# Spectral mixer and gated FFN on one core: remainder transform in 64 by 64 tiles, masked products on 128 partitions, a new middle order, and two weight slots loaded later

## Chip, core and metric

One core of a Trainium2 chip runs the whole program. The metric is the device time of one execution in microseconds. The kernel before ran three times: 489.95, 490.86 and 492.05 us, median 490.86. A fourth execution was profiled: 489.82 us, of which the span from its first to its last recorded instruction is 487.8 us. The granted TensorE clock was 1.000 throughout.

## What is computed

```
x = A_x                                    # 1 x 2048 x 576
X = rfft2(layernorm(x)) * (w_r + 1j*w_i)   # w: 2048 x 289
h = x + irfft2(X)
y = h + (gelu(n @ w_gate) * (n @ w_up)) @ w_down,   n = layernorm(h)
# w_gate, w_up: 576 x 4608, w_down: 4608 x 576; all bf16
```

## The kernel before

The token axis of 2048 is split as 128 by 16 in the program's Fourier transforms, the channel axis of 576 into halves, and every transform is a matmul with a constant table. The program is written by hand as one list of operations per engine; a small recorder (class Prog) keeps, for each operation, which keys it reads and writes, and from these it works out the semaphore waits. Each engine executes its list strictly in the order in which the operations were recorded. So the order of the calls in the source is the order on each engine.

The stages, with their times in the profiled execution:

1. *Start, to about 20 us.* x arrives, layernorm statistics, and a first token transform (line 552) into U.
2. *Middle, about 20 to 46 us.* The order is the string SEQF (line 28), a list of tokens with a letter and a group number 0 to 15. A capital letter is the first half of a step, the small letter its second half:
   - D/d, st_D (line 636): channel transform, U times FT into two PSUM banks (line 640), then copied to CUS.
   - B, st_B (line 655): combination matmuls (line 660), then copied to YS.
   - T, st_T (line 664): VectorE multiplies YS by the spectral weights WS: 256 columns into TP, the remaining 32 columns of each group into TR (line 673). Four groups share one TR buffer.
   - V/v, st_V (line 676): token transform of TP (line 681), then copied to V.
   - R/r, st_R (line 692): the same transform for the remainder of four groups, TR times VT (line 697). Its PSUM result is copied to RB by ScalarE, and VectorE then multiplies RB by a 0/1 mask MK into VR (line 711), so that each group's rows stand alone.
   DENG, BENG and VENG (lines 29 and 30) say for each group whether ScalarE, VectorE or both make the copy of D, B and V. Copies all stand in line 607. The 128-partition by 512-column PSUM banks are handed out in four pairs by a loop over SEQF (line 592).
3. *Inverse, about 46 to 59 us.* The order is the string SEQ (line 33). I/i (line 808) transforms V and VR over channels, E copies the result to GS, N/o (line 825) transforms over tokens, a adds the result to x in XO (line 831). Then the second layernorm of the first four token tiles: s, q, c, n (lines 834 to 858; the norms with the letter P run on GpSimd), u/U (line 877) turns the tile by a matmul with the unit matrix, e copies it to HT. G0 and G1 are the first matmuls of the FFN.
4. *FFN, from 58.61 us.* Four blocks of 512 tokens; in each, 36 columns of 128 hidden units (line 917, gate and up), Gelu on ScalarE, product on VectorE, and then the down product (line 1004). In the first block the inverse of the other eight token tiles is woven in (deferred, lines 962 and 979).

In stage 2 and 3 a matmul uses 64 contraction rows: two of them, on rows 0 to 63 and 64 to 127, write two different PSUM banks. The second half of a step swaps the rows and adds to the other bank, and so waits for the first half (halves, line 612).

The weights of gate and up lie in four slots of nine hidden columns (1152 units) each. wg_load (line 629) issues for one slot two DMAs of w_gate from GpSimd's queue and two of w_up from SyncE's queue, 1.18 MB and 0.15 MB each. Slot 0 is issued at line 750. Slots 1 and 2 use the space of WS and its copies, so they wait for the last multiplication of st_T; they are issued at line 772, in the program's order between the middle and the inverse. w_down follows on GpSimd's queue (line 946), slot 0 is loaded anew at line 1024 once its nine columns are done in the first block.

Of the kernel before, what the change touches and what calls it, by code (L numbers as in the profile page):

```python
# [7 lines left out]
ALU = mybir.AluOpType  # L8
# [18 lines left out]
ACT_TILES = tuple(int(w[1:]) for w in SEQ1 if w[0] == "Q")  # L27
SEQF = """D1 D0 d1 D2 d0 d2 B1 D4 B0 d4 D3 T1 B2 T0 d3 D5 V1 d5 T2 v1 D6 B3 d6 B4 V0 B5 T3 v0 D7 T4 D8 d7 B6 d8 V3 R0 T5 v3 T6 r0 V2 B7 v2 D9 V5 d9 D10 v5 d10 V4 B9 T7 D12 v4 d12 B8 D11 T9 B10 d11 R1 D13 T8 T10 r1 d13 D14 B11 V6 d14 V7 v6 v7 T11 B12 V8 D15 v8 B13 T12 d15 B14 T13 V9 v9 T14 R2 r2 B15 V10 V12 v10 V13 v12 R3 T15 r3 V11 v13 V14 v11 v14 V15 R4 v15 r4""".split()
VENG = [('act',), ('dve',), ('act',), ('act',), ('act', 'dve'), ('act', 'dve'), ('act', 'dve'), ('act', 'dve'), ('act',), ('act',), ('act',), ('act',), ('act',), ('act',), ('act', 'dve'), ('act', 'dve')]
DENG, BENG = ['act', 'act', 'dve', 'act', 'act', 'act', 'dve', 'act', 'dve', 'act', 'act', 'act', 'dve', 'act', 'act', 'dve'], ['act', 'act', 'act', 'act', 'act', 'act', 'act', 'act', 'act', 'act', 'act', 'act', 'act', 'act', 'act', 'act']  # L30
QR = ((0, 1), (1, 2), (2, 3), (3, 4), (4, 8), (8, 16))
# [298 lines left out]
def _build(nc, A_x, A_w_r, A_w_i, B_w_gate, B_w_up, B_w_down, out):  # L330
# [91 lines left out]
    def bank(b, p0=0, p1=128, c0=0, c1=512):  # L422
        return PS[p0:p1, b * 512 + c0:b * 512 + c1]
# [185 lines left out]

    turn_over = {}  # L610

# [80 lines left out]
    def st_R(q, second):  # L692
        js = [i for i in range(4 * q, 4 * q + 4) if i < LAST] if q < 4 else [LAST]
        g0, n, b0 = GORD[js[0]], len(js), FB["R", q]

        def mm(h, o, t_, first, last, after):
            return P.op(PE, lambda t: t.matmul(bank(b0 + o, 0, 128, 0, 128), TR[64 * h:64 * h + 64, q % 2, o, t_, :], VT[64 * h:64 * h + 64, 1 + o if q == 4 else 0, t_, :], start=first, stop=last),
                        r=[("TR", q % 2, j) for j in range(4)] + ["VT"], w=[("PS", b0 + o)], after=after)

        halves(("R", q), second, [[0, 1]] * 2, mm)  # L700
        if not second:
            return
        ev(ACT, RB[:, q % 2, :, :, :, :].rearrange("p t n o e -> p o (t n) e"), banks(b0, 2, 128).rearrange("p o (a e) -> p o a e", e=4),
           [("PS", b0), ("PS", b0 + 1)], [("RB", q % 2)])
        for u in range((n + 1) // 2):
            m = min(2, n - 2 * u)
            for t_ in range(2):
                dst = VR[64 * t_:64 * t_ + 64, :, g0 + 2 * u:g0 + 2 * u + m, :, :].rearrange("p n g o e -> p n g (o e)")
                src = RB[64 * u:64 * u + 64, q % 2, t_, :, :, :].rearrange("p n o e -> p n (o e)").unsqueeze(2).to_broadcast([64, NT, m, 8])
                msk = MK[64 * u:64 * u + 64, 0:m, :].unsqueeze(1).to_broadcast([64, NT, m, 8])  # L710
                P.op(DVE, lambda v, dst=dst, src=src, msk=msk: v.tensor_tensor(dst, src, msk, op=ALU.mult),  # L711
                     r=[("RB", q % 2), "MK"], w=[("V", GORD[i], 2 + t_) for i in js[2 * u:2 * u + m]])

# [57 lines left out]
    P.alias(sum(wkeys, []) + sum(dup, []), [("WG", j, k) for j in (1, 2) for k in range(4)])  # L771
    for j in range(1, 3):
        wg_load(j, j)
    P.alias(["FT", "BT", "VT"], [("HT", 0, i, k) for i in range(4) for k in range(5)])

    vmain = [("V", g, c) for g in range(NG) for c in range(2)]
    vtail = [("V", g, c) for g in range(NG) for c in range(2, 4)]
    vk = [vmain, vmain, vtail]
# [4 lines left out]
    for t, w in enumerate(SEQ):  # L783
# [12 lines left out]
        elif k == "G":  # L796
            ing = True
            assert not held & {0, 1}

    ends = {}  # L800

# [60 lines left out]
    def turn_dma(c):  # L862
# [3 lines left out]
        for k in range(5):  # L866
            P.dma(SP, HT[:, k, 128 * (c % 4):128 * (c % 4) + 128], HN[:, hs, 128 * k:128 * k + 128], f"tr{c}",
                  r=[("HN", hs, 0), ("HN", hs, 1)], w=[("HT", q % 2, c % 4, k)], transpose=True)

    def turn_mm(c, second):  # L870
        hs, b0, e = c % 4, SLOT["u", c], ends.setdefault(("u", c), [None, None])
        plan = ((3, 0), (4, 1)) if second else ((0, 2), (1, 3), (2, 4))
        for j, ks in enumerate(plan):
            for r, k in enumerate(ks):
                r0, a = 64 * r, b0 * 512 + 192 + 128 * k + 64 * r
                o = a // 512 - b0
                e[o] = P.op(PE, lambda t, r0=r0, k=k, a=a: t.matmul(PS[:, a:a + 64], HN[r0:r0 + 64, hs, 128 * k:128 * k + 128], IDT[r0:r0 + 64, r0:r0 + 64], start=True, stop=True),
                            r=[("HN", hs, 0), ("HN", hs, 1), "IDT"], w=[("PS", b0 + o)], after=[e[o]] if second and j == 0 else [])
# [50 lines left out]
    def gu_first(i):  # L929
        for a in range(4):  # L930
# [5 lines left out]
           "e": turn_ev, "G": gu_first}  # L936
    for w in SEQ:
        a = w[1:]
        RUN[w[0]](*((int(a[:-1]), a[-1]) if a[-1] in "ADSP" else (int(a),)))

    P.alias(ukeys + [("CU", a) for a in range(3)], [("WD", j) for j in range(8)])

# [136 lines left out]
```

## Time and profile before

| | us or share |
|---|---|
| median of three runs | 490.86 |
| profiled execution, its span | 489.82, 487.8 |
| TensorE busy | 479.1 (98%) |
| VectorE, ScalarE, GpSimd busy | 188.6, 147.2, 43.2 |
| first matmul of the inverse (line 808) | 46.24 |
| first residual add (line 831) | 49.74 |
| first FFN matmuls on the chain of waits (line 917) | 58.61 |
| last w_up part of slot 1: issue, landing | 44.81, 59.34 |
| last w_up part of slot 2: issue, landing | 46.23, 70.83 |
| first matmul that reads slot 1, slot 2 | 76.33, 95.30 |

Times are counted from the first recorded instruction. A matmul's busy time includes its way through the array, so that neighbours overlap: start to start says what the array is occupied for. A weight load (PEld) belongs to every matmul and runs beside the one ahead of it. "issue" as the cause of a wait is time in which the engine waited for nothing that the profile shows. In the profile's DMA part, queue q1 is the one that SyncE's issues go through, q0 that of GpSimd's, and the packets of kind "instruction" are the engines' own programs being fetched.

### The profile page before, as it was taken

How to read it: one execution, taken by the hardware profiler on the slowest of the kernel's cores; microseconds unless marked ns; L12 is line 12 of the kernel's file. 1: busy time of each engine (PE TensorE's matmuls, PEld its weight loads, DVE VectorE, ACT ScalarE, POOL GpSimd, SP SyncE). 2: the span in 40 equal slices, each digit the busy share in tenths (PEclk: the TensorE clock that was granted, in tenths of full speed). 3: DMA queues.
4: the chain of work that ended last, by engine and by line, in shares of the span. 5: the costliest groups of instructions: out<-in, count | busy, mean ns of one | idle time of the engine just before them, and what ended most of it. 6: DMA issues, size and time to landing. Idle time of an engine off the chain costs nothing.

```text
span 487.8 us, 10721 instructions
## 1 busy us (share of the span) xinstructions
PE 479.1 (98%) x4791; PEld 286.9 (59%) x4792; DVE 188.6 (39%) x389; ACT 147.2 (30%) x294; POOL 43.2 (9%) x77
## 2 busy tenths in 40 slices
PE   7998999999999999999999999999999999999998
PEld 3876675555577744444577644444677444444775
DVE  7898746666511134333311144333211233333011
ACT  6997754343400022233200022332100123323000
POOL 5852631000300000000000000000000000000000
PEclk9999999999999999999999999999999999999999
DMA  8969998211350000100000001000000000000000
GB/s 283 231 160 321 353 329 270 74 26 26 110 170 20 16 18 19 23 1 1 1 19 19 13 20 23 15 1 2 6 19 19 7 1 1 1 0 1 13 19 18
DMA packets 25533, 32.65 MB, mean 67 GB/s; under 512 B 11664, under 2 KB 18096, under 8 KB 25488
## 3 DMA queue, kind: packets, MB, share of 16 engines
q1 hardware_dynamic: 22048, 18.27, 13.0%
q0 software_dynamic: 3440, 13.70, 8.8%
q8 instruction: 37, 0.61, 0.5%
q14 instruction: 8, 0.07, 0.1%
HBM read 26.01 MB, written 2.36 MB: 58 GB/s over the span
## 4 chain that ended last, share of the span: by engine, by line
PE 91%; DVE 3%; DMA 2%; POOL 2%; ACT 1%; issue 1%; DVEq 0%; POOLq 0%
PE PS L917 57%; PE PS L1004 29%; PE PS L537 1%; DMA WS<-WS 1%; DVE TP L673 1%; DVE XO L831 1%; DMA WS<-in_A_w_r_dram 1%; ACT U L563 1%; PE PS L962 1%; POOL WS L725 1%; POOL WS L240 1%; PE PS L808 0%; DVE VR L711 0%; PE PS L979 0%; PE PS L825 0%
## 5 line engine op out<-in xcount | busy, mean ns | idle before, releaser
L917 PE MATMUL PS<-HT,WG 64*128 64x512 bf16 (+1 forms) x2142 | 233.5, 372 | 0.0
L917 PEld LDWEIGHTS PS<-HT,WG 64*128 64x128 bf16 x2142 | 109.8, 94 | 111.0 <-issue 0.9
L925 ACT ACTIVATE GL<-PS 128x512 bf16<-128x512 f32 x144 | 85.7, 596 | 282.4 <-PE PS L917 274.4
L926 DVE TENSOR_TENSOR AT<-GL,PS 128x512 bf16<-128x512 bf16 x144 | 98.8, 687 | 165.1 <-ACT GL L925 165.1
L1004 PE MATMUL PS<-WD,AT 128*128 128x288 bf16 (+2 forms) x1152 | 141.8, 286 | 0.0
L1004 PEld LDWEIGHTS PS<-WD,AT 128*128 128x128 bf16 x1152 | 111.0, 98 | 31.5 <-ACT GL L925 1.3
L1007 DVE TENSOR_TENSOR OS<-PS,XO 128x288 bf16<-128x288 f32 (+2 forms) x32 | 14.6, 458 | 123.3 <-PE PS L1004 123.3
L917 PE MATMUL PS<-HT,WGX 64*128 64x512 bf16 x486 | 53.4, 376 | 0.0
L917 PEld LDWEIGHTS PS<-HT,WGX 64*128 64x128 bf16 x486 | 23.7, 94 | 28.8
L640 PE MATMUL PS<-FT,U 64*128 64x288 bf16 x160 | 14.1, 284 | 0.3 <-DVE V L607 0.2
L834 ACT ACTIVATE OS<-XO,NM 128x576 bf16<-128x576 bf16 x14 | 10.8, 774 | 11.4 <-DVE XO L983 11.4
L681 PE MATMUL PS<-VT,TP 64*128 64x128 bf16 x256 | 11.2, 217 | 0.1
L673 DVE TENSOR_TENSOR TP<-YS,WS 128x1024 bf16<-128x1024 bf16 x16 | 11.0, 689 | 0.4 <-ACT YS L607 0.2
L240 POOL DMA_DIRECT2D WD<-in_B_w_down_dram x9 | 6.8, 759 | 49.1 <-PE PS L979 49.1
L563 ACT ACTIVATE U<-PS 128x384 bf16<-128x384 f32 (+2 forms) x31 | 10.5, 427 | 1.4 <-PE PS L552 1.3
L495 DVE BATCH_NORM_STATS2 ST<-XO 128x6 f32<-128x288 bf16 x26 | 10.0, 441 | 1.9 <-DMA XO<-in_A_x_dram 1.7
L607 ACT ACTIVATE YS<-PS 128x576 bf16<-128x576 f32 x16 | 10.1, 661 | 0.3 <-PE PS L660 0.2
L552 PE MATMUL PS<-ATS,XO 128*128 128x128 bf16 x96 | 8.1, 219 | 1.9 <-POOL ATS L521 1.7
L681 PEld LDWEIGHTS PS<-VT,TP 64*128 64x128 bf16 x256 | 8.4, 94 | 2.1 <-PE PS L681 0.2
L537 PE MATMUL PS<-ZD 128*128 128x512 bf16 x19 | 7.5, 560 | 1.5 <-POOL ZD L430 1.5
L552 PEld LDWEIGHTS PS<-ATS,XO 128*128 128x128 bf16 x96 | 6.9, 98 | 3.1 <-POOL ATS L521 2.5
L640 PEld LDWEIGHTS PS<-FT,U 64*128 64x128 bf16 x160 | 7.0, 94 | 2.7 <-DVE V L607 0.7
(83 smaller groups left out, 213.5 us busy)
## 6 DMA issues: line engine op xcount, KB each, us to landing
WD<-in_B_w_down_dram POOLq DMA_DIRECT2D x9, 576.0 KB, 13.1
WG<-in_B_w_gate_dram POOLq DMA_DIRECT2D x4, 1152.0 KB, 9.8
WG<-in_B_w_up_dram SPq DMA_DIRECT2D x4, 1152.0 KB, 9.4
out_dram<-OS SPq DMA_DIRECT2D x30, 72.0 KB, 1.6
XO<-in_A_x_dram SPq DMA_DIRECT2D x3, 576.0 KB, 7.2
WGX<-in_B_w_up_dram SPq DMA_DIRECT2D x1, 1152.0 KB, 5.6
WGX<-in_B_w_gate_dram POOLq DMA_DIRECT2D x1, 1152.0 KB, 9.9
HT<-HN SPq DMA_TRANSPOSE x60, 2.4
```

The source lines that it names most:

```text
L240: fn = lambda e: e.dma_start(out_ap, in_ap)
L537: P.op(PE, lambda t: t.matmul(bank(b), ZD[:, 0:128], ZD[:, :], start=True, stop=True), r=["ZD"], w=[("PS", b)])
L552: P.op(PE, lambda t, b=b, lhs=lhs, p0=p0, p1=p1, s=s, e=e, o=o, c=c: t.matmul(bank(b, p0, p1, o, o + 128), lhs, ATS[:, c, :], start=s, sto ...
L563: fn = (lambda v: v.tensor_copy(dst, src)) if eng == DVE else (lambda a: a.activation(dst, src, ACTF.Copy))
L640: return P.op(PE, lambda t: t.matmul(bank(b0 + o, 0, 128, 0, 2 * HK), U[64 * h:64 * h + 64, us, 2 * i:2 * i + 2, :, :], FT[64 * h:64 * h + ...
L673: P.op(DVE, lambda v, dst=dst, y4=y4, w4=w4: v.tensor_tensor(dst, y4, w4, op=ALU.mult), r=[("Y", sl), *dup[(i >= 5) + (i >= 8) + (i >= 12) ...
L681: return P.op(PE, lambda t: t.matmul(bank(b0 + o, 0, 128, 128 * c, 128 * c + 128), TP[64 * h:64 * h + 64, z, o, t_, c:256:2], VT[64 * h:64 ...
L917: op = P.op(PE, lambda t, h0=h0, kt=kt, wt=wt, b=b, s=(not second and j == 0), e=(second and j == n - 1): t.matmul(bank(b, 0, 128, c0, c1) ...
L925: P.op(ACT, lambda a: a.activation(GL[:, s2, :], bank(b0), ACTF.Gelu_apprx_tanh), r=[("PS", b0)], w=[("GL", s2)])
L926: P.op(DVE, lambda v: v.tensor_tensor(AT[:, f, :], GL[:, s2, :], bank(b0 + 1), op=ALU.mult), r=[("GL", s2), ("PS", b0 + 1)], w=[("AT", f)])
L1004: P.op(PE, lambda t, b=b, d0=d0, d1=d1, f=f, p=p: t.matmul(bank(b, 0, 128, 0, d1 - d0), AT[:, f, 128 * p:128 * p + 128], WD[:, f, d0:d1], ...
L1007: P.op(DVE, lambda v, b=b, d0=d0, d1=d1, p=p, c=c: v.tensor_tensor(OS[:, p % 2, d0:d1], bank(b, 0, 128, 0, d1 - d0), XO[:, c, d0:d1], op=A ...
```

## The change

- *Remainder transform.* st_R no longer multiplies 64 rows by 128 columns of TR: each of its matmuls becomes four, with 64 columns of TR (u) by 64 of VT (z), each writing 64 partitions and 64 columns of its bank: the block of u and z goes to partition half z and column half u, where it went to partition half u and column half z before. 8 matmuls per step become 32. So the two token halves z of a pair of groups stand on the two partition halves, as in VR.
- *Masked products.* Therefore line 711, which made one product per pair of groups and token half on 64 partitions, makes one per pair on 128 partitions. Two keys per group of VR become one.
- *Order.* SEQF, VENG, DENG and BENG are new. SEQ is the same.
- *Loads.* Slots 1 and 2 are issued behind the whole list SEQ, and SyncE and GpSimd first wait for the last TensorE operation recorded ahead of G0. On GpSimd the three norms of SEQ then stand ahead of these loads, on SyncE the order is the same.

```diff
--- before.py
+++ after.py
@@ -25,9 +25,9 @@
 LORD = "x0-2 x2-4 a0-4 x4-8 a4-8 x8-12 x12-16 a8-16".split()
 SPLIT = tuple(int(w[1:-1]) for w in SEQ1 if w[0] == "F")
 ACT_TILES = tuple(int(w[1:]) for w in SEQ1 if w[0] == "Q")
-SEQF = """D1 D0 d1 D2 d0 d2 B1 D4 B0 d4 D3 T1 B2 T0 d3 D5 V1 d5 T2 v1 D6 B3 d6 B4 V0 B5 T3 v0 D7 T4 D8 d7 B6 d8 V3 R0 T5 v3 T6 r0 V2 B7 v2 D9 V5 d9 D10 v5 d10 V4 B9 T7 D12 v4 d12 B8 D11 T9 B10 d11 R1 D13 T8 T10 r1 d13 D14 B11 V6 d14 V7 v6 v7 T11 B12 V8 D15 v8 B13 T12 d15 B14 T13 V9 v9 T14 R2 r2 B15 V10 V12 v10 V13 v12 R3 T15 r3 V11 v13 V14 v11 v14 V15 R4 v15 r4""".split()
-VENG = [('act',), ('dve',), ('act',), ('act',), ('act', 'dve'), ('act', 'dve'), ('act', 'dve'), ('act', 'dve'), ('act',), ('act',), ('act',), ('act',), ('act',), ('act',), ('act', 'dve'), ('act', 'dve')]
-DENG, BENG = ['act', 'act', 'dve', 'act', 'act', 'act', 'dve', 'act', 'dve', 'act', 'act', 'act', 'dve', 'act', 'act', 'dve'], ['act', 'act', 'act', 'act', 'act', 'act', 'act', 'act', 'act', 'act', 'act', 'act', 'act', 'act', 'act', 'act']
+SEQF = """D0 D2 d0 D1 d2 d1 B0 T0 D5 B2 d5 D3 B1 d3 D4 V0 T2 T1 d4 v0 D6 B3 d6 B4 D7 B5 T3 d7 V1 T4 D8 v1 d8 V3 T5 V2 v3 v2 B7 D10 B6 d10 R0 T7 T6 V5 r0 v5 D9 B10 d9 D11 B8 d11 D13 B9 d13 V4 D12 v4 T8 B11 T10 d12 D14 B13 T9 d14 V6 R1 v6 T11 r1 B12 V8 D15 v8 d15 T13 V7 V9 v7 T12 R2 v9 r2 V13 B14 v13 T14 V10 B15 V12 v10 T15 v12 V11 V14 v11 v14 V15 R3 v15 R4 r3 r4""".split()
+VENG = [('dve',), ('act',), ('act',), ('act', 'dve'), ('act',), ('act',), ('act', 'dve'), ('act',), ('act',), ('act', 'dve'), ('act',), ('act', 'dve'), ('act',), ('act', 'dve'), ('act', 'dve'), ('act', 'dve')]
+DENG, BENG = ['act', 'dve', 'act', 'act', 'act', 'act', 'dve', 'act', 'act', 'dve', 'act', 'dve', 'dve', 'act', 'act', 'act'], ['act', 'act', 'act', 'act', 'act', 'act', 'act', 'dve', 'act', 'act', 'act', 'act', 'act', 'act', 'act', 'act']
 QR = ((0, 1), (1, 2), (2, 3), (3, 4), (4, 8), (8, 16))
 DEF0, DSTEP = 3, 4
 SEQ = """I3 I1 i3 I2 E3S i1 i2 E1S N3 I0 o3 i0 a3 N1 E2A N2 E0S o1 I7 a1 s3A o2 N0 i7 o0 q3 s1A a2 c3 I5 a0 E7A s2D I6 q1 i5 E5A c1 s0D i6 E6A N7 I4 o7 n3P i4 q2 a7 n1P u3 q0 N5 U3 E4A c0 o5 e3A c2 u1 n2P U1 e1A N6 n0D u0 o6 U0 N4 a5 u2 e0A a6 U2 o4 G0 e2D a4 G1""".split()
@@ -607,7 +607,7 @@
         fn = (lambda v: v.tensor_copy(dst, src)) if eng == DVE else (lambda a: a.activation(dst, src, ACTF.Copy))
         P.op(eng, fn, r=r, w=w)
 
-    turn_over = {}
+    turn_over, ends = {}, {}
 
     def halves(key, second, plans, mm):
 
@@ -693,23 +693,26 @@
         js = [i for i in range(4 * q, 4 * q + 4) if i < LAST] if q < 4 else [LAST]
         g0, n, b0 = GORD[js[0]], len(js), FB["R", q]
 
-        def mm(h, o, t_, first, last, after):
-            return P.op(PE, lambda t: t.matmul(bank(b0 + o, 0, 128, 0, 128), TR[64 * h:64 * h + 64, q % 2, o, t_, :], VT[64 * h:64 * h + 64, 1 + o if q == 4 else 0, t_, :], start=first, stop=last),
-                        r=[("TR", q % 2, j) for j in range(4)] + ["VT"], w=[("PS", b0 + o)], after=after)
-
-        halves(("R", q), second, [[0, 1]] * 2, mm)
+        e = ends.setdefault(("R", q), [[None, None], [None, None]])
+        for t_ in range(2):
+            for u in range(2):
+                for z in range(2):
+                    for h in range(2):
+                        o, r0, z0 = h ^ second, 64 * h, 64 * z
+                        e[o][z] = P.op(PE, lambda t, o=o, r0=r0, z0=z0, t_=t_, u=u: t.matmul(bank(b0 + o, z0, z0 + 64, 64 * u, 64 * u + 64), TR[r0:r0 + 64, q % 2, o, t_, 64 * u:64 * u + 64],
+                                                                                             VT[r0:r0 + 64, 1 + o if q == 4 else 0, t_, z0:z0 + 64], start=(not second and t_ == u == 0), stop=(second and t_ == u == 1)),
+                                       r=[("TR", q % 2, j) for j in range(4)] + ["VT"], w=[("PS", b0 + o)], after=e[o] if second and t_ == u == z == 0 else [])
         if not second:
             return
-        ev(ACT, RB[:, q % 2, :, :, :, :].rearrange("p t n o e -> p o (t n) e"), banks(b0, 2, 128).rearrange("p o (a e) -> p o a e", e=4),
+        ev(ACT, RB[:, q % 2, :, :, :, :].rearrange("p u n o e -> p o (u n) e"), banks(b0, 2, 128).rearrange("p o (a e) -> p o a e", e=4),
            [("PS", b0), ("PS", b0 + 1)], [("RB", q % 2)])
         for u in range((n + 1) // 2):
             m = min(2, n - 2 * u)
-            for t_ in range(2):
-                dst = VR[64 * t_:64 * t_ + 64, :, g0 + 2 * u:g0 + 2 * u + m, :, :].rearrange("p n g o e -> p n g (o e)")
-                src = RB[64 * u:64 * u + 64, q % 2, t_, :, :, :].rearrange("p n o e -> p n (o e)").unsqueeze(2).to_broadcast([64, NT, m, 8])
-                msk = MK[64 * u:64 * u + 64, 0:m, :].unsqueeze(1).to_broadcast([64, NT, m, 8])
-                P.op(DVE, lambda v, dst=dst, src=src, msk=msk: v.tensor_tensor(dst, src, msk, op=ALU.mult),
-                     r=[("RB", q % 2), "MK"], w=[("V", GORD[i], 2 + t_) for i in js[2 * u:2 * u + m]])
+            dst = VR[:, :, g0 + 2 * u:g0 + 2 * u + m, :, :].rearrange("p n g o e -> p n g (o e)")
+            src = RB[:, q % 2, u, :, :, :].rearrange("p n o e -> p n (o e)").unsqueeze(2).to_broadcast([128, NT, m, 8])
+            msk = MK[:, 0:m, :].unsqueeze(1).to_broadcast([128, NT, m, 8])
+            P.op(DVE, lambda v, dst=dst, src=src, msk=msk: v.tensor_tensor(dst, src, msk, op=ALU.mult),
+                 r=[("RB", q % 2), "MK"], w=[("V", GORD[i], 2) for i in js[2 * u:2 * u + m]])
 
     def dup_w(k, jp, pl=slice(0, 2), eng=None):
         a, b = 64 * jp, 64 - 64 * jp
@@ -769,12 +772,10 @@
 
 
     P.alias(sum(wkeys, []) + sum(dup, []), [("WG", j, k) for j in (1, 2) for k in range(4)])
-    for j in range(1, 3):
-        wg_load(j, j)
     P.alias(["FT", "BT", "VT"], [("HT", 0, i, k) for i in range(4) for k in range(5)])
 
     vmain = [("V", g, c) for g in range(NG) for c in range(2)]
-    vtail = [("V", g, c) for g in range(NG) for c in range(2, 4)]
+    vtail = [("V", g, 2) for g in range(NG)]
     vk = [vmain, vmain, vtail]
     vkeys = vmain + vtail
 
@@ -797,8 +798,6 @@
             ing = True
             assert not held & {0, 1}
 
-    ends = {}
-
     def i_mm(c, second):
         b, e = SLOT["I", c], ends.setdefault(("I", c), [None, None])
         for j in range(2 + second):
@@ -866,6 +865,8 @@
         for k in range(5):
             P.dma(SP, HT[:, k, 128 * (c % 4):128 * (c % 4) + 128], HN[:, hs, 128 * k:128 * k + 128], f"tr{c}",
                   r=[("HN", hs, 0), ("HN", hs, 1)], w=[("HT", q % 2, c % 4, k)], transpose=True)
+
+    gate_op = []
 
     def turn_mm(c, second):
         hs, b0, e = c % 4, SLOT["u", c], ends.setdefault(("u", c), [None, None])
@@ -935,9 +936,15 @@
            "s": lambda c, e: sq(c, ENG[e]), "q": ln2_q, "c": ln2_c, "n": lambda c, e: norm(c, ENG[e]), "u": lambda c: turn_mm(c, False), "U": lambda c: turn_mm(c, True),
            "e": turn_ev, "G": gu_first}
     for w in SEQ:
+        if w == "G0":
+            gate_op.append(P.ops[PE][-1])
         a = w[1:]
         RUN[w[0]](*((int(a[:-1]), a[-1]) if a[-1] in "ADSP" else (int(a),)))
 
+    for eng in (SP, POOL):
+        P.op(eng, None, after=[gate_op[0]])
+    for j in range(1, 3):
+        wg_load(j, j)
     P.alias(ukeys + [("CU", a) for a in range(3)], [("WD", j) for j in range(8)])
 
     def wd_load(j):
```

## Prediction

> **What bounds the kernel now.** I read the page first, then the chain of waits, then two windows of it instruction by instruction.
>
> The page: TensorE carries the run, and most of it lies in two lines that never wait.
>
> ```profile
> q8 instruction: 37, 0.61, 0.5%
> ...
> L917 PE MATMUL PS<-HT,WG 64*128 64x512 bf16 (+1 forms) x2142 | 233.5, 372 | 0.0
> ...
> L1004 PE MATMUL PS<-WD,AT 128*128 128x288 bf16 (+2 forms) x1152 | 141.8, 286 | 0.0
> ```
>
> The last number is idle time before the group: 0.0. From 58.61 us on the chain of waits is these two lines and the deferred columns, back to back, until 485.55. So the change can move only the start of that stretch, unless a weight comes late in it. Everything is decided before 58.61.
>
> The chain between 43 and 59 us (start, length, what):
>
> ```profile
> 43.52 0.70 DVE TP L673
> ...
> 45.36 0.75 DVE V L607 x2
> 46.10 0.14 issue
> 46.24 1.89 PE PS L808 x28
> 48.13 0.54 issue
> 48.67 0.30 PE PS L808 x2
> ...
> 49.74 0.76 DVE XO L831
> ...
> 55.55 0.62 DVE HN L858 x2
> ...
> 58.61 1.41 PE PS L917 x23
> ```
>
> VectorE ends the middle (46.10), TensorE begins the inverse (46.24), and from 49.74 to 56.17 VectorE works without a hole. What moves the first residual add (49.74) moves 58.61, and the end, by as much. The edits have to be priced at that add. "issue" at 48.13 is a stall with no semaphore behind it.
>
> The window 20.09 to 46.24 (sum, then busy time of PE, PEld, DVE, ACT, POOL, clock, DMA share, GB/s):
>
> ```profile
> 20.09:46.24 26.15, 24.76 (x522) 18.58 (x521) 25.03 (x66) 24.41 (x52) 11.97 (x22) 1.00 0.82 233
> ```
>
> Three engines are full at once. VectorE has 1.1 us of holes.
>
> **VectorE and ScalarE in the middle.** Line 711 ran 18 times on 64 partitions, 14 of 256 elements (0.284 us) and 4 of 128 (0.22): 4.86 us. On 128 partitions there are 7 and 2, 2.43 us, if the time goes by elements in a partition: TR on 128 partitions (128x128) takes 0.220, VR on 64 (64x128) 0.221. So -2.43. The new engine lists put one YS copy on VectorE (+0.76, as its 128x576 CUS copies) and split seven V copies, not six (+0.42). Net -1.25 us. ScalarE: one YS (0.66) and one whole V (0.60) less, one half V (0.42) more: -0.84.
>
> **TensorE in the middle.** 40 matmuls of line 697 become 160 of 64x64. A call of four took 0.112 us (34.527 to 34.639). The nearest row is line 877, whose moving side also has 64 columns: a pair each 0.0285, so 16 in 0.23. Bounds: four tiles at once, 0.11; one after the other as in line 552 (0.056 each), 0.90. I take 0.23: +0.12 on each of 10 calls, 1.2. A change of array shape shows three times: 19.943 to 20.095 where the spacing was 0.055, 133.411 to 133.720 for 0.216, 168.888 to 169.106 for 0.122, each about 0.10 more. The new order has eight stretches of these calls, 16 changes: 1.5. So +2.7 us of TensorE; ends 0 and 9.4.
>
> [...]
>
> So work that VectorE loses (1.25) comes back on TensorE, whose starts alone (160 and 64 matmuls at 0.061, 296 at 0.028) already take 22.0 us of 26.15.
>
> **The instruction blocks.** Each added matmul also brings a weight load: 240 more TensorE instructions ahead of the inverse. The 37 packets of q8 hold 16,384 bytes each. Laid beside the trace, one belongs to every 256 TensorE instructions; block limits fall at 192 + 256 n in the count of executed instructions. The stall at 48.13 ends exactly on such a limit (number 1472), and that instruction has no wait in the program. Packet times against the instant when TensorE passes a limit: 29.11, packet 31.08; 35.37, 38.85; 41.68, 46.05; 48.66, 52.55; in the quiet dense part the packet comes 1.9 us before. So with full DMA queues (1.00 from 40 to 44 us) a packet is 3.5 to 4.4 us late; it takes 1.2 and TensorE resumed 1.43 after it: 6.2 to 7.0 us from one limit until the next block can run. Before, a block lasted 6.3 us (22.68, 29.11, 35.37, 41.68): just enough, and once not.
>
> [...]
>
> After, limits fall by the built order as follows. T8 still waits for its copied weights (landed 34.40), so the ninth T starts at 34.45 as before. Limit 960 lies ahead of it, in V4 and D12, about 33.9. Limit 1216 lies in v7, which T12 needs. VectorE from 34.45: five T (0.75 each), one CUS copy (0.76), half a V (0.42), two VR (0.57): T12 at 39.95. The block behind 1216 is asked for at 33.9 and there at 40.1, so v7 runs then and T12 slips to about 40.4. Limit 1472 lies in v11, three calls behind v10, which T15 needs. From T12 to T15 VectorE has T12 and T14 (1.5), two half V (0.84), two VR (0.57): T15 at 43.3, v11 due about 44. But the block asked for at 40.1 is there at 46.3 to 47.1: a stall of 2.3 to 3.1 us where nothing is buffered any more. The weights moved away don't help: their issue was at 44.39. From v11 to the first inverse matmul are 184 instructions with V15, v15 and four R calls: 1.9 us by the same end of before (44.37 to 46.24), plus 0.3 for two shape changes. Inverse at 48.5 to 49.3. The next limit, 1728, falls about 2 us into the inverse; its packet is asked for at about 46.7 with the queue nearly empty (what is left of slot 0's weights and two tables landed by 49.35 even with the later weights in between), so I take no stall, where before had 0.54. Add at 46.24-to-49.74 without the stall, 2.96 later: 51.5 to 52.3 against 49.74, +1.8 to +2.5. I take the low end, **+1.8**, since the packet is late by 3.5 more often than by 4.4.
>
> **Weights of slots 1 and 2 behind the inverse.** Eight issues (SP 3.3 us, POOL 2.7) go from 44.39 to the last matmul ahead of G0, about 58.4. On POOL the three norms now go ahead of them; in before the first norm waited 5.2 us for VectorE, not for POOL, so that is worth 0. Behind the new wait stand, on SP, these loads, the reload of slot 0 (78.61) and the transposes (94.69); on POOL w_down's eight loads (5.9 us of issue) and line 848, whose result the norm at 94 needs: free by 68. Slot 1 took 14.95 us (44.39 to 59.34) in a full queue: from 58.4 that is 73.4, needed at 76.33 (first matmul of column 9), both shifted alike. Slot 2 landed at 70.83, needed at 95.30. In all 5.3 MB and 4.7 MB of w_down at 354 GB/s (70 to 75 us) are done near 89; w_down is first read at 133.8, slot 3's reload at 114.0. Cost 0; cover 2.9 us.
>
> **Sum.** Profiled execution 489.82 (span 487.8, 2.0 around it) + 1.8 = 491.6. It lay 1.04 under the median of the three runs, so on that scale 490.86 + 1.8 = **492.7**; the times below are on it too.
>
> **Rivals.**
> - *Both gains arrive.* If blocks are there in time, VectorE's 1.25 less ends the middle at 45.0 and the 0.54 goes too: -1.8 at best, and TensorE's 2.7 takes part of it: -0.7 to -1.8, 489.1 to 490.2. It needs packets late by under 2 us, as the one at 31.08 was. For it: three of the four blocks of the middle were in time before. Against: the last of these by 0.1 (38.85, 1.3 and 1.43 make 41.6, limit at 41.68), and queues are as full as before until 44. [...] 25%.
> - *Even.* TensorE's drains take what VectorE gives, and one block stalls by as much as before: -0.7 to +0.7, 490.2 to 491.6. 17%.
> - *Tiles one after the other.* 0.90 a call makes TensorE +9.4; with 22.0 us of starts it is 31 in 26, so the inverse slips by 3 to 5 us: 494 to 496. It decides from about 0.35 a call. For it: no 64*64 row exists. Against: pairs on two row groups start 3.4 ns apart. 9%.
> - *Slot 1 late.* With both queues full the packets of SP's queue moved 96 to 138 GB/s (52 to 60 us). Its 1.33 MB for slot 1 at 96 take 13.9, with 2 to start: 74.3, in time by 2. Behind 76.33 each us counts in full: +1 to +4. 5%.
> - *The edit doesn't act*: the built order shows norms ahead of loads on POOL and SP's order unchanged but for the wait, so at most the move is idle, and the middle decides as above.
>
> **Numbers.** Main case (blocks late) 44%, 491.5 to 494.2. A difference under 0.5% (2.45 us) is about what a measurement of this kernel can't tell from none. Beyond it upward: a fifth of the main case, the tiles, most of the late slot, 0.22. Beyond it downward would need more than everything that stands before 49.74: 0.03. Range 489.2 to 495.2 leaves out about 15%.
>
> **What would show it.** Right: TensorE idle for 2 to 3 us with "issue" among the V matmuls near 44, on instruction 1472; no "issue" near 48; first L917 matmul near 60.2; DMA share low from 50 to 58. Wrong: first inverse matmul ahead of 46, or 64*64 calls far from 0.23 us, or idle time at L917 released by a DMA near 77.

## The result and the profile after

Twelve executions of the changed kernel: 492.34 to 496.69 us, median **494.57**. Twelve of the kernel before on the same chip: median 490.94; one of these took 718.17 us and is not in the ratio. The ratio is 1.0072, 95% interval 1.0050 to 1.0094: the change costs 3.6 us, 0.7%. The profiled execution took 494.01 us with a span of 492.2 (before: 489.82 and 487.8).

The lines of the page that answer to the first three of before (idle before a group is the last number):

```profile
q8 instruction: 38, 0.62, 0.5%
...
L918 PE MATMUL PS<-HT,WG 64*128 64x512 bf16 (+1 forms) x2142 | 233.5, 372 | 0.0
...
L1011 PE MATMUL PS<-WD,AT 128*128 128x288 bf16 (+2 forms) x1152 | 141.8, 286 | 0.0
```

The FFN takes the same time as before and still waits for nothing, so no weight came late. One more block of instructions was fetched. The loss lies ahead of the FFN. The chain of waits between 39 and 63 us (start, length, what):

```profile
39.42 0.47 PE PS L681 x16
39.88 2.37 issue
42.26 0.40 PE PS L681 x8
...
44.22 0.85 PE PS L681 x16
...
45.55 2.11 PE PS L681 x46
47.67 1.48 issue
49.15 0.68 PE PS L681 x18
...
51.35 2.01 PE PS L807 x30
...
54.14 0.76 DVE XO L830
...
59.95 0.63 DVE HN L857 x2
...
63.01 3.04 PE PS L918 x53
```

The reader is to see two things. The first residual add stands at 54.14 against 49.74, and the FFN starts at 63.01 against 58.61: both 4.40 us later, and the span grew by 4.4. And the word "issue" stands twice in the middle, 2.37 and 1.48 us. In the trace these two stalls end on TensorE's executed instructions 1217 and 1473, one behind the block limits 1216 and 1472. The second of these instructions has no semaphore wait. The first waits for the first half of its own step on TensorE, and that semaphore had come at 39.88, when the stall began; it does not explain the 2.37 us behind it.

TensorE's own waits between 20 and 62 us (engine, line, releaser: sum, times, longest) say the same, no other engine holds it up for long:

```profile
PE PS L681 <- issue: 3.9, 2, 2.4
PE PS L878 <- DVE HN L857: 0.8, 1, 0.8
```

Between the two stalls something else is to be read. Windows of one microsecond (busy time of PE, PEld, DVE, ACT, POOL, then granted clock, DMA share, GB/s):

```profile
42.00:43.00 1.00, 0.74 (x30) 0.60 (x32) 0.30 (x1) 0.30 (x1) 0.00 (x0) 1.00 1.03 347
43.00:44.00 1.00, 1.00 (x36) 0.70 (x32) 0.87 (x4) 0.95 (x3) 0.00 (x0) 0.88 1.08 402
44.00:45.00 1.00, 1.00 (x20) 0.99 (x18) 0.81 (x3) 0.74 (x2) 0.00 (x0) 0.50 1.04 389
45.00:46.00 1.00, 1.00 (x20) 0.83 (x18) 0.84 (x3) 0.59 (x2) 0.00 (x0) 0.50 1.12 369
46.00:47.00 1.00, 1.00 (x24) 1.00 (x22) 0.48 (x1) 0.80 (x3) 0.00 (x0) 0.50 1.05 191
47.00:48.00 1.00, 0.67 (x20) 0.54 (x15) 0.35 (x2) 0.53 (x2) 0.00 (x0) 0.92 0.92 284
```

The granted clock is 0.50 from 43.76 to 47.17, 1.5 us after the first stall ended. TensorE is "busy" all the time, but 16 matmuls of line 681 take 0.85 us at 44.22 where they took 0.47 at 39.42: their pairs start 0.106 us apart instead of 0.053 to 0.056. A share of busy time does not show this; the clock column does. (The counts of 36 and 20 are not to be compared: 16 of the 36 are the small matmuls of line 702.)

The 4.40 us at the add: +2.37 and +1.48 (stalls), about +1.4 (half clock, priced below by a kernel made for it), -0.54 (the stall of before near 48, gone). That makes 4.7; by this account the rest is 0.3 us shorter. This trace has one half-clock stretch and a mean clock of 0.997, as seven of the twelve executions have; the other five have 0.993, as have the traces of e2 and e7 below, whose half clock lasts twice as long. The medians of the two kinds are 493.47 and 495.21, so 494.57 mixes them.

The packets of the instruction queue, from the trace (us). "Behind by" counts from the instant when TensorE executes past the limit; "held" means that the pass itself came after a stall:

| limit | before: passed, packet, behind by | after: passed, packet, behind by |
|---|---|---|
| 704 | 29.11, 31.08, 1.97 | 29.41, 29.93, 0.52 |
| 960 | 35.37, 38.85, 3.48 | 34.80, 39.65, **4.85** |
| 1216 | 41.68, 46.05, 4.37 | 42.26 (held), 46.50, **4.24** |
| 1472 | 48.66, 52.55, 3.89 | 49.15 (held), 50.31, 1.16 |

TensorE ran from limit 960 to 1216 in 6.31 us before and in 5.08 after (34.80 to 39.88): the calls of 64 by 64 tiles hold four times as many instructions in nearly the same time (16 matmuls start within 0.126 us, a call of four took 0.112).

### The profile page after: what moved, and what is told of

It is laid out like the page before. It is cut to its first block, busy times and chain, and to the rows that moved or that the text cites. A ratio compares the mean times of both kernels' runs of the same rounds, so it can differ in the third digit from the quotient of the medians.

```text
span 492.2 us, 10953 instructions
## 1 busy us (share of the span) xinstructions
PE 480.6 (98%) x4912; PEld 288.8 (59%) x4912; DVE 186.9 (38%) x382; ACT 147.5 (30%) x293; POOL 43.1 (9%) x77
## 4 chain that ended last, share of the span: by engine, by line
PE 92%; DVE 2%; issue 1%; ACT 0%; DVEq 0%
PE PS L918 57%; PE PS L1011 29%; PE PS L681 2%; PE PS L640 2%; PE PS L660 1%; DVE XO L830 1%; PE PS L969 1%; PE PS L807 0%; PE PS L986 0%; PE PS L824 0%; PE PS L702 0%; DVE OS L892 0%; PE PS L878 0%; DVE CUS L607 0%; DVE HN L857 0%
## 5 line engine op out<-in xcount | busy, mean ns | idle before, releaser
L681 PEld LDWEIGHTS PS<-VT,TP 64*128 64x128 bf16 x256 | 9.4, 105 | 5.5 <-issue 4.2
L607 ACT ACTIVATE V<-PS 128x512 bf16<-128x512 f32 (+1 forms) x15 | 7.1, 497 | 5.0 <-PE PS L681 5.0
```

Of the source, the lines that this page charges most:

```text
L607: fn = (lambda v: v.tensor_copy(dst, src)) if eng == DVE else (lambda a: a.activation(dst, src, ACTF.Copy))
L681: return P.op(PE, lambda t: t.matmul(bank(b0 + o, 0, 128, 128 * c, 128 * c + 128), TP[64 * h:64 * h + 64, z, o, t_, c:256:2], VT[64 * h:64 ...
```

## Experiments

Twelve kernels ran. The **theory**: TensorE's next block of 256 instructions arrives late while slot 0's weights fill the DMA queues, and the added instructions carry TensorE to the limit sooner. The **rivals**: the tiles themselves cost the time, with what is lost at a change of the array's shape (called drains in the prediction and the expectations; what the trace of before has of it are three gaps of 0.09 to 0.10 us); the new order does; the moved loads do. Times are medians on their own chip; ratios are to the kernel before, measured with it there.

| | ratio, 95% interval | median us (before) | first add, profiled |
|---|---|---|---|
| e1_loads | 1.0002, 0.9991 to 1.0014 | 489.94 (490.27) | 49.66 |
| e2_tiles | 1.0109, 1.0094 to 1.0125 | 495.43 (490.27) | 54.71 |
| e3_order | 1.0019, 1.0007 to 1.0031 | 490.98 (490.27) | 51.67 |
| e4_after_slot0 | 0.9959, 0.9946 to 0.9971 | 488.18 (490.27) | 49.54 |
| e5_before_slot0 | 0.9974, 0.9961 to 0.9988 | 489.19 (490.50) | 49.41 |
| e6_order_slot0 | 1.0010, 0.9996 to 1.0023 | 490.80 (490.50) | 53.11 |
| e7_split | 1.0123, 1.0100 to 1.0146 | 496.40 (490.50) | 56.12 |
| e8_tiles_slot0 | 0.9969, 0.9954 to 0.9984 | 488.43 (490.50) | 48.47 |
| e9_pause_short | 0.9987, 0.9974 to 1.0000 | 489.10 (490.26) | 49.18 |
| e10_pause_long | 1.0032, 1.0016 to 1.0048 | 491.75 (490.26) | 51.77 |
| e11_gate_late | 1.0065, 1.0048 to 1.0082 | 493.24 (490.26) | 53.38 |
| e12_up_late | 1.0002, 0.9990 to 1.0014 | 489.89 (490.26) | 49.25 |

The profiled execution is one of many, and its start alone differs by up to a microsecond or two (e6's, 493.35 us against a median of 490.80, had the clock at half from 13.5 to 16.9 us, before any edited line; its add is not compared).

### The parts alone

e1: the kernel before, and of the change only the later issue of slots 1 and 2.

```diff
-    for j in range(1, 3):
-        wg_load(j, j)
...
+    for eng in (SP, POOL):
+        P.op(eng, None, after=[gate_op[0]])
+    for j in range(1, 3):
+        wg_load(j, j)
```

> The kernel before with one part of the change: the loads of slots 1 and 2 go behind the inverse list. Theory (instruction blocks come late while slot 0, the tables and the copied weights fill the DMA queues): nothing differs before 44.39 us, so the block limit 1472 still stalls TensorE near 48 by 0.3 to 0.6 us; no other stall; total -0.5 to +0.2 us against before. Rival 'the moved loads cost' : slot 1 or the blocks in the FFN come late behind them, +1 to +4 us, seen as idle time of the gate and up matmuls.

e2: the kernel before with only st_R and its keys as in the change.

```diff
-        halves(("R", q), second, [[0, 1]] * 2, mm)
+        for t_ in range(2):
+            for u in range(2):
+                for z in range(2):
+                    for h in range(2):
...
+            P.op(DVE, lambda v, dst=dst, src=src, msk=msk: v.tensor_tensor(dst, src, msk, op=ALU.mult),
+                 r=[("RB", q % 2), "MK"], w=[("V", GORD[i], 2) for i in js[2 * u:2 * u + m]])
```

> The kernel before with the 64 by 64 remainder transform and the 128-partition masked products alone; old order, old engine lists, old loads. Theory: 240 more TensorE instructions put two block limits into the stretch from 34 to 46 us while the queues are full; stalls of 1 to 2.5 us each without a semaphore, on instruction counts 192 + 256 n, a TensorE clock at half for some microseconds if a stall exceeds 2 us: +1.5 to +4 us. Rival 'drains of the array': no such stalls, only some 0.2 us at each of the calls, 0 to +1.5 us. Rival 'the order is to blame': -1 to 0 us, VectorE being relieved by 2.4.

e3: the kernel before with only the new strings and lists.

```diff
-SEQF = """D1 D0 d1 D2 d0 d2 B1 D4
...
+SEQF = """D0 D2 d0 D1 d2 d1 B0 T0
...
```

> The kernel before with the new order of the middle and the new engine lists alone; 128-column remainder matmuls, half-partition products, old loads. Theory: no instruction added, so blocks last as long as before; at most the one stall of before: -0.5 to +1.0 us. Rival 'the order is to blame': +2.5 to +4 us.

The loads cost nothing (1.0002). One thing in e1 was not as expected: its trace has no stall at limit 1472, and its first inverse matmuls run through (46.88 to 48.89). The packet came 3.12 us behind limit 1216, where it was 4.37 before. Whether the moved loads or chance did this can't be told from one trace; no gain shows in the median. The order alone costs 0.2%, as expected. The tiles alone cost 5.2 us, above the 1.5 to 4 expected and more than the whole change. So the loss is in the tiles' part, and the question is by which way. The chain of e2 between 40 and 55 us:

```profile
39.60 0.42 issue
40.02 0.29 PE PS L640
...
44.00 3.02 issue
47.02 0.26 PE PS L702 x3
47.29 2.67 PE PS L681 x36
...
54.71 0.76 DVE XO L832
```

Both stalls end on a limit again (1216 and 1472), in another order of the work. In this trace the clock is 0.5 from 45.61 to 52.44.

### The queues quiet

e4: the changed kernel with slot 0's load (and the two tables behind it) issued after VectorE's last token product.

```diff
-    wg_load(0, 0)
...
+            if w == "T15":
+                slot0_op.append(P.ops[DVE][-1])
...
+    for eng in (SP, POOL):
+        P.op(eng, None, after=[slot0_op[0]])
+    wg_load(0, 0)
```

> The changed kernel whole, with slot 0's loads and the two small tables behind them (2.65 and 0.5 MB) issued only after the last spectral product (T15) instead of at 32 to 42 us. Theory: the queues empty by about 40 us and the instruction packets come in time; the stalls at counts 1216 and 1472 shrink from 2.4 and 1.5 us to under 0.7 together and the clock stays at full, so the inverse begins near 45 us and the total is 1 to 2.5 us under before (3.5 to 6 under the changed kernel). Slot 0 lands near 55 us, needed at 57. Rivals 'drains' and 'order': total stays 2 to 4 us over before.

It is the fastest kernel of the study: 0.9959, 2.1 us under the kernel before and some 5 under the changed one. With both queues quiet the packets follow limits 960, 1216 and 1472 by 0.59, 0.50 and 0.66 us. The next, after limit 1728 (48.85), falls into the load of slot 0 (44.84 to 56.91) and is 3.93 behind again; there a block lasts 8 us, and nothing waits. Its chain, at the place where the changed kernel stood still:

```profile
40.35 0.69 PE PS L681 x24
...
43.19 2.04 PE PS L681 x64
...
46.75 2.01 PE PS L812 x30
...
49.54 0.76 DVE XO L835
```

The group that broke off after 16 matmuls runs through with 24, and the one of 46 and 18 with 64. From the start of that group to the add are 9.19 us; in the changed kernel 14.72 (39.42 to 54.14). Slot 0 lands at 56.91, 1.5 us before the first gate product (58.41).

e5: the kernel before with the edits of e1 and of e4, slots 1 and 2 and slot 0 issued late. e6: e5 with the new order (the edit of e3). e8: e5 with the tiles (the edit of e2), in the old order. What e5 changes:

```diff
-    wg_load(0, 0)
...
+    for eng in (SP, POOL):
+        P.op(eng, None, after=[slot0_op[0]])
+    wg_load(0, 0)
...
-    for j in range(1, 3):
-        wg_load(j, j)
...
+    for eng in (SP, POOL):
+        P.op(eng, None, after=[gate_op[0]])
+    for j in range(1, 3):
+        wg_load(j, j)
```

> The kernel before with the loads of slots 1 and 2 behind the inverse stage and with slot 0 (and the two small tables behind it on SyncE's queue) issued only after the last token product of VectorE. No tiles, old order. Theory of the queues (instruction packets are late because slot 0's load fills the DMA queues): the packets in the middle follow their limits by under 1 us instead of 3.1 to 4.4, but the kernel before lost only 0.54 us to a wait for instructions, so at most that comes back: ratio 0.998 to 1.000, 489.3 to 490.3. Rival (slot 0 early is a load that takes bandwidth from the middle in general, or is needed early): faster by over 1.5 us, or slower since the first gate products wait for slot 0.

> The changed kernel with slot 0 issued late as in e4, but without the tiles and without the masked products on all partitions: new middle order, loads behind the inverse stage, old remainder. It is e4 less its tiles part. Theory (with quiet queues the tiles and the masked products are worth what the chain of the middle gives back, some tenths of a microsecond to 1): between 488.2 and 489.5, e4 at 488.2 a little below it. Rival (the slot 0 move is the whole gain and the tiles cost even with quiet queues, some 1 to 2.7 us of TensorE time): 486 to 487.5, well below e4.

> The kernel of e2 (tiles and masked products alone, old order) with the loads of slots 1 and 2 behind the inverse stage and slot 0 late. Theory (e2 lost its 5 us to late instruction packets): without slot 0 in the queues the waits of 3.0 and 0.4 us and the stretch at half clock go, and the time is that of e4 or a few tenths above, 488.0 to 489.6. Rival (the tiles themselves cost in the old order): 491 or more.

e5 is faster than before by 1.3 us, just past its expected range (0.9974 against 0.998 to 1.000). At most 0.5 of it is the stall of before; e5 stands 0.28% under e1, and where the other 0.8 or more comes from was not settled. It also means that most of e4's gain does not come from the tiles and the order: against e5, which has the same late loads, e4 is 0.15% faster, some 0.7 us, and the two intervals overlap. e8 came out as the theory had it: the same tiles that cost 5 us with a full queue cost nothing measurable with a quiet one (e8 against e5: 0.9969 and 0.9974). e6 missed both expectations: the new order without the tiles is slower than the old one, 1.0010 against 0.9974. So the order and the tiles belong together: in the new order the tiles are worth 0.5% (e6 to e4). e4 and e8 can't be told apart.

### Instructions or drains

e7: the kernel before, each remainder matmul in four of 32 columns, the shape of the array unchanged. TensorE gets exactly as many instructions more as by the tiles, and no new change of shape.

```diff
-            return P.op(PE, lambda t: t.matmul(bank(b0 + o, 0, 128, 0, 128), TR[64 * h:64 * h + 64, q % 2, o, t_, :], VT[64 * h:64 * h + 64, 1 + o if q == 4 else 0, t_, :], start=first, stop=last),
...
+            for c in range(0, 128, 32):
+                op = P.op(PE, lambda t, c=c: t.matmul(bank(b0 + o, 0, 128, c, c + 32), TR[64 * h:64 * h + 64, q % 2, o, t_, :], VT[64 * h:64 * h + 64, 1 + o if q == 4 else 0, t_, c:c + 32], start=first and c == 0, stop=last and c == 96),
...
+            return op
```

> The kernel before with each matmul of the remainder's token transform split into four matmuls of 32 columns in the same array shape: 120 matmuls and 120 weight loads more, as many more instructions as the 64 by 64 tiles add, with no change of the array's shape. Theory (the count of instructions moves the limits of the blocks in front of their packets, which are late while slot 0 loads): TensorE waits for instructions for 2 to 4 us in all, at executed counts 1216, 1472 or 1728 exactly, and a long wait is followed by some 3 us at half clock: 492.5 to 495.5. Rival (the loss of the tiles is the drains at the shape changes and the tiles' own time): no such wait, only the streaming of 120 more matmuls, at most 1.5 us: 490.0 to 491.8.

496.40 us: the loss of e2 without a tile and without a new change of shape. It is somewhat above the range expected, and the chain shows the stall that is the reason:

```profile
44.16 0.23 PE PS L698 x16
...
44.44 0.36 PE PS L698 x13
44.80 3.83 issue
48.63 0.18 PE PS L698
```

It ends on instruction 1473; one of 0.43 us ends on 1217. The clock was 0.5 from 46.34 to 53.17. That the number of instructions is a way to the whole loss is shown; with e8, where the tiles and their shape changes cost nothing measurable, these changes are refuted as its cause.

### The half clock alone

e9 and e10: e4 with TensorE held ahead of v7, by two or four memsets of an unused tile on GpSimd. No late packet, no load.

```diff
+            if w == "v7":
+                prev = P.ops[PE][-1]
+                for _ in range(2):
+                    prev = P.op(POOL, lambda g: g.memset(ZD[:, :], 0.0), w=["ZD"], after=[prev])
+                P.op(PE, None, after=[prev])
```

> The kernel of e4 (the changed kernel with slot 0 late: no waits for instructions, clock 1.00) with a pause put into TensorE's stream ahead of the second half of the token product v7, near the place of the changed kernel's first stall: TensorE waits for two memsets of GpSimd of 0.53 us each, about 1.2 us. The memsets write zeros to a tile that nothing reads any more. Theory (an idle TensorE of some 2.4 us is answered by a stretch at half the granted clock, a short one is not): at most the pause itself, 488.3 to 489.5, with the granted clock at 1.00 in the microseconds after it. Rival (each idle microsecond is paid with more than itself, whatever its length): over 489.7.

> As the one with the short pause, but four memsets: about 2.3 us of an idle TensorE, as long as the changed kernel's first stall, with quiet DMA queues and no late instruction packet. Theory (the pause alone brings the stretch at half clock): the granted clock falls to 0.5 for about 3 us, some 4 us after the pause began, and the time grows by the pause and about 1.5 us: 491.0 to 492.5. Rival (the half clock of the changed kernel came from something else, the loads or the tiles): at most the pause, 489.5 to 490.6, clock 1.00.

Windows of e10 (columns as above); the clock in e9's profile is 1.00 throughout:

```profile
40.00:41.00 1.00, 0.00 (x0) 0.00 (x0) 0.00 (x0) 0.00 (x0) 0.89 (x3) 1.00 0.00 0
...
43.00:44.00 1.00, 1.00 (x22) 0.85 (x18) 0.69 (x4) 0.71 (x2) 0.00 (x0) 0.52 0.00 0
44.00:45.00 1.00, 1.00 (x19) 0.83 (x16) 1.00 (x3) 0.59 (x3) 0.00 (x0) 0.50 0.00 0
45.00:46.00 1.00, 1.00 (x26) 1.00 (x22) 0.32 (x2) 0.80 (x2) 0.00 (x0) 0.50 0.00 0
46.00:47.00 1.00, 1.00 (x32) 0.98 (x30) 0.60 (x2) 0.78 (x2) 0.10 (x1) 0.78 0.06 16
```

The DMA share is 0.00 and the clock is halved all the same: the pause alone does it. From the start of the same group to the add e9 takes 10.58 us (38.60 to 49.18) and e10 13.09 (38.68 to 51.77). Against e4's 9.19 that is +1.39 for a pause of 1.2 and +3.90 for one of 2.4: some 0.2 in both, and 1.3 to 1.4 for the clock. e10's twelve runs show it a second time. Nine have a mean clock of 0.996 or 0.997 and a median of 491.85; three kept 1.000 and took 490.19 to 490.37. So the half clock, where it comes, costs **1.6 us**, and after 2.4 us of idle it comes mostly, not always.

The clock's records say more. The half-clock stretches last 3.413 us or twice that, and their starts lie on one grid of 3.413 us in each run. For some windows of this grid the table gives TensorE's busy share and its work: rows by columns by elements of each matmul that starts in the window, summed, where 128 by 128 by one element counts as 1.

| kernel | window | busy share | work | clock in the next window |
|---|---|---|---|---|
| e11 | 43.32 to 46.73 | 0.30 | 1632 | 0.5 |
| e6 (start) | 10.10 to 13.51 | 0.35 | 2048 | 0.5 |
| after | 40.35 to 43.76 | 0.44 | 2336 | 0.5 |
| e10 | 39.63 to 43.04 | 0.44 | 2480 | 0.5 |
| e2 | 42.20 to 45.61 | 0.51 | 2640 | 0.5 |
| e7 | 42.93 to 46.34 | 0.53 | 2768 | 0.5 |
| after (second stall) | 47.17 to 50.59 | 0.57 | 3040 | 1.0 |
| after (start) | 9.62 to 13.04 | 0.44 | 3072 | 1.0 |
| before (start) | 10.71 to 14.12 | 0.51 | 3328 | 1.0 |
| e12 | 36.65 to 40.06 | 0.68 | 4320 | 1.0 |
| e9 | 37.03 to 40.44 | 0.64 | 4448 | 1.0 |

Busy share alone doesn't decide: among the middle's windows at full clock 0.53 and less brought the half clock and 0.57 and more did not, but in the start, where matmuls are larger (128 rows, not 64), windows of 0.44 and 0.51 kept 1.0. The work sorts them: in the ten traces that hold clock records, every window followed by half clock has at most 2768, and every window followed by full clock at least 3040. The sorting was made after the runs, and none was built to test it. By it the place of a pause in the grid would decide whether one window loses enough: the grid starts elsewhere in each run (first record at 4.65 to 7.29 us). That would fit the three executions of e10 that kept their clock, but they have no trace. None of the windows in the table that were followed by half clock was idle: they were 30 to 53% busy.

### Which half of slot 0

e11 holds back only the gate half of slot 0 (GpSimd's queue) in the changed kernel, e12 only the up half and the two tables (SyncE's).

```diff
-    wg_load(0, 0)
+    wg_load(0, 0, (1,))
...
+    P.op(POOL, None, after=[slot0_op[0]])
+    wg_load(0, 0, (0,))
```

The new last argument names the halves, 0 for gate and 1 for up; these are e11's lines, and e12 has the two exchanged and SP for POOL.

> The changed kernel with only the gate half of slot 0 (GpSimd's queue, issued at 32.8 in the changed kernel, landed from 40.5) held back to the last token product; the up half and the two small tables go out early as in the changed kernel (issued at 39.1, landed from 46.9). Theory (each half of slot 0 makes the packet late that is asked for while it loads): the packet after limit 960 is there within about 2 us and the stall of 2.4 us and the half clock go; the packet after limit 1216, due by about 44.5, is still held up by the up half, a stall of 0.5 to 1.5 us: 488.8 to 490.2. Rival (only the sum of the loads matters, or the loads move up and do the same harm): 491.5 or more.

> The changed kernel with only the up half of slot 0 (SyncE's queue) and the two small tables held back; the gate half goes out early as in the changed kernel. Theory (each half its own stall): the stall of about 2.4 us at count 1216 and the half clock after it stay, the one of 1.5 us at count 1472 goes: 491.8 to 493.3. Rival (the up half makes both): 488.0 to 489.5.

Both missed their theory's range, by 3 us up and 2 down, and the two come out in the opposite order. e11's 493.24 lies in the range of its rival (491.5 or more); the up half landed at 45.50 and 47.88, some 1.5 and 2 us earlier than in the changed kernel (46.95 and 49.87). e12's 489.89 lies 0.4 above that of its rival. The chain of e11, and then that of e12:

```profile
42.12 1.49 PE PS L682 x46
43.61 2.38 issue
...
51.72 1.07 issue
...
53.38 0.76 DVE XO L836
```

```profile
38.51 0.47 PE PS L682 x16
38.97 1.38 issue
40.35 0.40 PE PS L682 x8
...
49.25 0.76 DVE XO L836
```

The place was as expected, but for the second stall of e11: with the up half early (landing to 47.9) the limits 1472 and 1728 stall, with the gate half early (landing to 40.6) the limit 1216. So the rival that the up half makes both stalls is refuted. The sizes were not. The up half alone makes 2.38 us at 1472, where I had 0.5 to 1.5, and the half clock followed it (46.73 to 50.14). The gate half alone makes 1.38 at 1216, where I had 2.4, and no half clock followed (a mean clock of 1.000 in all twelve executions). As between e9 and e10, 1.2 us more of a pause make 2.5 us more of time. Why limit 960's packet was 4.85 us behind with both halves and 3.97 with the gate half alone was not separated from the spread of single traces.

## Why the prediction came out as it did

The main case, blocks late, is what happened; the time, 494.57, lies 1.9 us over its 492.7 and 0.4 over the 494.2 up to which that case went. One of its terms was far too small (+1.9), one was missing (+1.4), and one came out too large (-0.8): together +2.5 at the first add, which stood at 54.14 and not at 51.5. The last follows from the first two, which had delayed the work in front of that limit. That the errors partly cancel is why the time ends only 0.4 above the case.

- **Stall at limit 1216: mis-sized.** "There at 40.1, due 39.95": a slip of some tenths. Measured 2.37, so that the 2 to 3 us of "issue" named as a sign came one limit earlier than named. TensorE came to the limit at 39.88, as predicted. But limit 960 was passed at 34.80, not 33.9, and the block could run 7.46 us after it, where I had 6.2 to 7.0. I had taken the low end of the bounds at the very place where supply and need were 0.15 us apart. The reason given, late by 3.5 "more often than by 4.4", isn't in the four packets listed (1.97, 3.48, 4.37 and 3.89 behind): here it was 4.85.
- **Half clock: missing.** About 1.4 us. All that the trace of before showed from 7.29 us to the end of the FFN was 1.00, and no "issue" stall of TensorE in its middle or inverse was longer than 0.54.
- **Stall at limit 1472: mechanism and price right, size moved.** From the instant the block was asked for to its first instruction, 6.2 to 7.0 us were predicted and 6.9 measured (42.26 to 49.15). It cost 1.48 and not 2.3 to 3.1, since the first stall and the half clock had already delayed the work in front of it (47.67 where 44 was due).
- **No stall near 1728: right.** The packet for it came at 50.31, 1.16 us after limit 1472 was passed, and 1728 was reached at 53.45. **The stall of before gone: right,** but it is gone in e1 too, without a gain in e1's median. From the first inverse matmul to the add 2.79 us, predicted 2.96.
- **Tiles: a little too dear.** The 16 matmuls of a call start within 0.126 us (30.944 to 31.070), where I had 0.23 for a call and bounds of 0.11 and 0.90; four tiles start 3 to 4 ns apart and the next four 0.022 to 0.042 us after them, so the four go together and not one after the other. Into the tiles a change of shape adds about 0.09, and 0.125 go from the last start of a call to the next matmul, where I had 0.10 for each, taken over from three gaps between other shapes. Such a call takes 0.34 with both, where a call of four took 0.11: some 1.9 over the eight stretches, instead of 2.7.
- **Masked products: right.** Seven at 287 ns and two at 218 make 2.45 us, predicted 2.43. With 256 elements in a partition a product took 287 ns on 128 partitions and 284 on 64, with 128 elements 218 and 220: here the time went by elements in a partition.
- **Weights behind the inverse: right at 0** (e1, 1.0002). Slot 1 landed at 75.56 and was needed near 80.7 (76.33 and the 4.40 later start): 5 us of cover, predicted 2.9.
- **The rivals.** "Both gains arrive" is the way of e4, where the packets are in time: 0.9959, on the scale of the prediction 488.8, against 489.1 to 490.2. But e5 has most of that gain without the tiles and the new order, and what is left for these, about 0.7 us, is the low end of this rival's 0.7 to 1.8 and not clear of noise. "Tiles one after the other" and "slot 1 late" did not happen. "Even" did not either; e12, with one stall of 1.38, comes nearest (1.0002).

TensorE passes its limits without a stall in e4, where the packets follow three of them by 0.50 to 0.66 us, and in the dense part, where they come early (by 1.3 to 2.1 us in before from 155 us on). Under a full queue it stalled for 2.37 and 1.48 us (after), 3.02 (e2) and 3.83 (e7).

Still open: what in a full queue holds the packet back (its place behind other packets on the DMA engines was inferred from the times, not shown), why e5 gained 0.8 us or more beyond the stall of before, and why the new order without the tiles is slower than the old one with quiet queues (e6 against e5).

## What to carry to other kernels

When an edit splits matmuls, count the instructions: TensorE's program came in DMA packets of 256 instructions (16,384 bytes), these came up to 4.9 us behind their limits here while loads filled the queues, and a stretch that ran through a block in 5.1 us stood still at the limit where one of 6.3 mostly did not. Read "issue" on the chain, the clock and the DMA share together, and move a load that isn't needed yet out of that stretch before judging the edit: that turned a loss of 0.7% into a gain of 0.4%, of which the move of the load alone gives 0.26% (e5). Price a pause of TensorE with what follows it: here 1.2 us cost 1.4, 2.4 us cost up to 3.9.

## What the runs showed of the hardware

- Eleven stalls, in six kernels (before among them), end on instruction 1216, 1472 or 1728 or one behind it, whatever line stands there. They last 0.16 to 3.83 us. Each ends 1.2 to 1.7 us after the end of the packet that followed the limit before (after: limit 960 at 34.80, packet 39.65 to 40.86, running at 42.26). So no stall shows more than one block held ahead.
- The granted clock changes on a grid of 3.413 us whose place differs from run to run (first record at 4.65 to 7.29 us): windows with a work of at most 2768 (128 by 128 by one element is 1) were followed by 0.5, those with 3040 and more were not, and the busy share alone does not sort them (0.44 stands on both sides). A pause of 2.4 us with a DMA share of 0.00 is enough for the half clock in nine of twelve executions; these nine took 1.6 us longer in the median than the other three (e10).
- Sixteen matmuls of 64*64 with 64 columns start within 0.126 us, each four within 0.010; about 0.09 us are lost into that shape, and 0.125 pass from its last start to the next matmul.
